# Where a unit's maxima are rounded, and when a weight may be split

## The chip, the cores and the metric

The kernel runs on one core of one Trainium2 chip. The metric is the device time of one execution in microseconds (us). Before the change three runs took 2253.95 us in the median (2253.94 to 2255.15).

The core's engines run side by side, each through its own queue in order. The profile calls them PE (TensorE, matrix products), PEld (its weight loads), DVE (VectorE), ACT (ScalarE), POOL (GpSimd) and SP (SyncE, which issues most transfers here).

## The reference

One input `x` of 2048 tokens by 576 goes through two branches whose results a gate mixes:

```python
g = sigmoid((x * gate_w).sum(-1, keepdims=True))
# branch A: attention with 32 heads of 18
q, k, v = split(x @ wqkv)
p = softmax(q @ k.T * 18 ** -0.5)          # per head, 2048 x 2048
a = concat(p @ v) @ wo
# branch B: a feed-forward block of width 4608
h = gelu(layernorm(x) @ w1 + b1)           # the tanh form of GELU
b = h @ w2 + b2
out = g * a + (1 - g) * b
```

All of it is float32. TensorE multiplies in a shorter float32 form here (`F32R`), so the kernel carries most operands as two parts: `hi`, the value rounded to that form, and `lo`, the remainder `value - hi`. A product is then hi x hi + hi x lo + lo x hi. Making the two parts of a weight is called splitting it.

## The kernel before

After a first stage (projections of q, k, v; layer norm; about the first 250 us) one long loop runs. It weaves attention and feed-forward together on TensorE.

**Attention.** Two heads make a pair, half of the queries of a pair make a unit: 32 units, each of 16 steps `kc` over the keys. Before a unit's scores can go through the exponential, the maximum of each query's scores must be known. So every unit is gone through twice. In *rounds* (`s1_round`, 32 to a unit, lines 204 and 206) TensorE makes scores and VectorE reduces each 128x512 bank to its maxima (tile `m4`). When a unit's last round has been issued, `s1_finish` (lines 209 to 237 with its inner `rows`) reduces the maxima once more to 128x16 negated values `nm` (line 215), makes the rounded part `nmh` (216), copies it beside the remainder into `nm2` (217, 218), and two slots later `rows` transposes `nm2` (222) and stores it in two extra rows of the unit's query tile `qa`. The second pass (`s2`, line 279) multiplies with those rows, so that scores come out with the maximum taken off, and ScalarE puts them through `Exp` (line 281). `s2` works in half-steps: two score matmuls, one for each head, into a pool `ps_s2` of two banks, and two exponentials that empty them. `pv` (line 308) multiplies the probabilities with v. Rounds run ahead of `s2`: a unit's rounds are done some four steps (a step is about 3.7 us) before its own second pass begins.

**Feed-forward.** Tokens are worked in four blocks of 512, and for each block the width in 36 chunks of 128, as 18 pairs, nine groups of two pairs. `h_pair` (matmuls of line 547) makes a pair's hidden values, which then go through GELU in pieces on three engines: ScalarE and VectorE empty the banks (572, 571), ScalarE squares (635), GpSimd multiplies (line 160, a helper through which all GpSimd arithmetic of the loop goes), ScalarE takes the tanh (628), GpSimd multiplies again, rounds (tile `hh`) and makes the remainder (tile `hl`). `open_pairs[0]` is 1 from the end of a pair's matmuls until the last of these instructions has been issued; the last matmul of the next pair isn't issued before (line 559). `out_pair` (matmuls of line 679) multiplies with `w2` and VectorE adds the results up (653). The order of a group is: first pair, the outputs of the group before, second pair, and so on.

**Weights.** In the first token block, w1 and w2 come from memory and are split on the way: ScalarE copies into the rounded part (line 444), GpSimd subtracts (line 160, tile `w`), and both parts are stored to scratch memory for the three later blocks, which only load them. `split` appends a job to the list `bg`. w1 comes as 128x1152 per pair through one raw buffer, w2 as 128x576 per chunk through four. After a split the next raw load is issued three slots later.

**What sets the order.** Nothing reorders the instructions; each engine runs what was issued in the order of the program text. A planner in the text decides that order: `run_due` advances a slot, with an estimated time (`now[0]`), issues what was deferred to this slot (`later`, `timed`), and then looks through `bg`: a job starts when GpSimd's estimated backlog is under its bound (one slot's 950 ns for w1, four for w2) and its `due()` is reached, which among other things is no earlier than 12 slots after a w1 load. `fill` puts feed-forward matmuls between half-steps and then calls `run_due`. A round normally runs inside a half-step of `s2`; `lend_round` runs it inside an output tile instead (within a fill), and the next half-step then has none. `take_round` defers `s1_finish` by one slot.

## Time and profile before

| | before |
|---|---|
| median of three runs | 2253.95 us |
| the profiled execution | 2255.1 us, span 2253.3 us |
| busy: PE, DVE, ACT, POOL | 99%, 74%, 64%, 42% of the span |
| granted clock of TensorE | 0.998 |

The span is the stretch from the first to the last instruction of one profiled execution. A row of a timeline reads: start in us, how long in us, engine, line (L281 is line 281 of the kernel), operation, tiles written and read, shape, how many were merged, and in brackets how long the engine stood still before it and what ended that. A row of grouped instructions has the count behind an x, then busy us, mean ns of one, idle us before them. A busy TensorE is not TensorE at its peak, and idle time of an engine that others don't wait for costs nothing.

### The profile page before, as it was taken

The page shows a single profiled execution, that of the slowest core. Times are in us where ns is not written, and L with a number is a line of the kernel's source. Part 1 is how long each engine was busy: PE and PEld are TensorE (multiplying, and loading weights), DVE is VectorE, ACT ScalarE, POOL GpSimd, SP SyncE. Part 2 cuts the span into 40 slices and gives each one's busy share as a digit, 9 for nine tenths or more (in the row PEclk, how much of TensorE's full clock was granted, in tenths as well). Part 3 has the DMA queues.
Part 4 walks back from the last instruction along what each step waited for, and adds up shares of the span by engine and source line. Part 5 has one row for each costly group of instructions (what it writes and reads, how often), then busy time and mean ns, then how long its engine had stood idle before and what let it go on. Part 6 is the DMA issues. An engine that isn't in the chain of part 4 may idle for free.

```text
span 2253.3 us, 51099 instructions
## 1 busy us (share of the span) xinstructions
PE 2231.5 (99%) x20569; PEld 1649.5 (73%) x20569; DVE 1671.8 (74%) x2953; ACT 1431.6 (64%) x2623; POOL 946.2 (42%) x936
## 2 busy tenths in 40 slices
PE   8999999999999999999999999999999999999999
PEld 7878766777777777777777777777777777777769
DVE  5675877777787787778777877787778777877545
ACT  4223677777776666666666666666666666666661
POOL 4002466666664444443444344434444444444420
PEclk9999999999999999999999999999999999999999
DMA  7755655545473424243264424243465233323355
GB/s 244 261 189 184 193 164 164 173 131 163 133 223 137 149 98 126 98 128 108 89 177 153 120 97 131 90 122 120 122 167 159 98 120 115 106 99 115 109 177 193
DMA packets 163218, 323.61 MB, mean 144 GB/s; under 512 B 59646, under 2 KB 86178, under 8 KB 152146
## 3 DMA queue, kind: packets, MB, share of 16 engines
q1 hardware_dynamic: 158982, 313.57, 44.0%
q10 hardware_dynamic: 4000, 6.78, 0.8%
q8 instruction: 162, 2.65, 0.5%
q14 instruction: 74, 0.61, 0.1%
HBM read 229.07 MB, written 95.16 MB: 144 GB/s over the span
## 4 chain that ended last, share of the span: by engine, by line
PE 92%; POOL 3%; DVE 2%; ACT 2%; DMA 1%; issue 0%; SPq 0%; ACTq 0%; DVEq 0%; POOLq 0%
PE ps L308 20%; PE ps L679 19%; PE ps L547 18%; PE ps L279 14%; PE ps L204 11%; PE ps L955 4%; PE ps L1263 3%; PE ps L973 2%; POOL zz L160 1%; POOL hl L160 1%; POOL w L160 1%; DVE m L206 1%; PE ps L870 0%; DMA p<-in_A_wqkv_dram 0%; ACT p L281 0%
## 5 line engine op out<-in xcount | busy, mean ns | idle before, releaser
L206 DVE TENSOR_REDUCE m<-ps 128x1 f32<-128x512 f32 x2048 | 1301.1, 684 | 299.6 <-PE ps L204 254.4
L281 ACT ACTIVATE p<-ps 128x512 f32<-128x512 f32 x1368 | 743.5, 596 | 377.5 <-PE ps L204 231.3
L279 PE MATMUL ps<-qa,ka 56*128 56x512 f32 x2048 | 715.1, 414 | 4.8 <-ACT p L281 3.8
L204 PE MATMUL ps<-ka,qa 54*128 54x512 f32 x2048 | 647.2, 418 | 3.8 <-DVE m L206 2.6
L679 PE MATMUL ps<-w,hh 64*128 64x288 f32 x4352 | 526.2, 296 | 2.4 <-ACT z L572 1.6
L279 PEld LDWEIGHTS ps<-qa,ka 56*128 56x128 f32 x2048 | 359.8, 185 | 229.6 <-issue 113.5
L547 PE MATMUL ps<-big,w 64*128 64x512 f32 x3888 | 513.9, 390 | 0.2 <-ACT vt L984 0.2
L160 POOL TENSOR_SCALAR zz<-zz 128x512 f32<-128x512 f32 x272 | 168.8, 621 | 776.5 <-ACT zz L635 693.9
L281 ACT ACTIVATE ring<-ps 128x512 f32<-128x512 f32 x680 | 369.6, 596 | 190.4 <-PE ps L204 124.9
L547 PEld LDWEIGHTS ps<-big,w 64*128 64x128 f32 x3888 | 401.6, 185 | 51.9 <-ACT vt L984 0.4
L679 PEld LDWEIGHTS ps<-w,hh 64*128 64x128 f32 x4352 | 421.7, 186 | 15.9 <-ACT z L572 2.1
L160 POOL TENSOR_TENSOR zz<-zz,z 128x512 f32<-128x512 f32 x280 | 361.4, 1291 | 34.5 <-ACT zz L637 10.5
L679 PE MATMUL ps<-w,hl 64*128 64x288 f32 x2176 | 364.8, 292 | 0.0
L204 PEld LDWEIGHTS ps<-ka,qa 54*128 54x128 f32 x2048 | 333.5, 185 | 30.0 <-DVE m L206 10.4
L308 PE MATMUL ps<-p,vt 128*32 128x512 f32 x2736 | 344.5, 598 | 0.0
L679 PEld LDWEIGHTS ps<-w,hl 64*128 64x128 f32 x2176 | 246.4, 185 | 1.4
L160 POOL TENSOR_TENSOR w<-x,w 128x576 fp32r<-128x576 f32 (+1 forms) x34 | 69.0, 2033 | 295.7 <-ACT w L444 276.5
L308 PEld LDWEIGHTS ps<-p,vt 128*32 128x32 f32 x2736 | 71.4, 109 | 153.9 <-issue 147.9
L308 PE MATMUL ps<-ring,vt 128*32 128x512 f32 x1360 | 179.1, 598 | 0.0
L160 POOL TENSOR_TENSOR hl<-zz,hh 128x512 fp32r<-128x512 f32 x134 | 172.5, 1287 | 15.2 <-ACT hh L598 4.3
L653 DVE SCALAR_TENSOR_TENSOR x<-ps,x 128x288 f32<-128x288 f32 x270 | 110.8, 452 | 83.3 <-PE ps L679 80.9
L955 PE MATMUL ps<-big,wqk 128*128 128x512 f32 x504 | 121.5, 396 | 0.4 <-ACT wqk L863 0.4
(118 smaller groups left out, 1382.8 us busy)
## 6 DMA issues: line engine op xcount, KB each, us to landing
w<-w_scr SPq DMA_DIRECT2D x54, 1152.0 KB
w<-w_scr SPq DMA_DIRECT2D x108, 576.0 KB
w_scr<-w SPq DMA_DIRECT2D x18, 1152.0 KB
w_scr<-w SPq DMA_DIRECT2D x36, 576.0 KB
qa<-qk_scr SPq DMA_DIRECT2D x192, 72.0 KB
ka<-qk_scr SPq DMA_DIRECT2D x90, 144.0 KB
x<-in_B_w_dram SPq DMA_DIRECT2D x34, 288.0 KB
qk_scr<-hh SPq DMA_DIRECT2D x36, 256.0 KB
```

Of the source, the lines that this page charges most:

```text
L160: fn(*args, **kw)
L204: nc.tensor.matmul(ps, qa[r0:r0 + 54, t * P:(t + 1) * P], ka[r0:r0 + 54, kb * TB:(kb + 1) * TB], start=True, stop=True)
L206: nc.vector.tensor_reduce(M4[u][:, h, t, kb:kb + 1], ps, axis=AX.X, op=ALU.max)
L279: nc.tensor.matmul(ps, ka[r0:r0 + 56, kc * P:(kc + 1) * P], qa[r0:r0 + 56, qb * TB:(qb + 1) * TB], start=True, stop=True)
L281: nc.scalar.activation(RING[n % 3][:, qb, h], ps, AF.Exp, scale=SCALE)
L308: nc.tensor.matmul(OB[u][r:r + 32, :], v[:, k, 19 * h:19 * h + 32], RING[c % 3][:, qb, h, :], start=(k == 0), stop=(k == NT - 1))
L547: nc.tensor.matmul(ps[h], wt[w_][r, c, :], Y[s_][r, c, :], start=(k == 0), stop=(k == 26))
L653: nc.vector.scalar_tensor_tensor(dst, ps[nn][:, :ND], 0.5, b2b[:, cs[nn]] if base else dst, op0=ALU.mult, op1=ALU.add)
L679: mm = nc.tensor.matmul(ps[nn][:, :ND], h_[r, tok], w_[p_][r, cs[nn]], start=(k == 0 or bare and k == 3 * G), stop=(k == 6 * G - 1 or bare ...
L955: nc.tensor.matmul(ps, w_[:, c, ms], big[:, s_, :], start=(k == 0), stop=(k == len(prods) - 1))
L973: nc.tensor.matmul(ps[:, :ND], big[:, s_, tok], w_[:, c, cs], start=(k == 0), stop=False)
L1263: nc.tensor.matmul(ps[t, n][:, :ND], OT[b][3][:, s_, tok], w_part(w_, c)[:, cs], start=(c == 0 and k == 0), stop=(c == 4 and k == 1))
```

## The change

Two things are edited. In `s1_finish`, the rounding of the maxima and the copy into `nm2` go from VectorE to ScalarE; ScalarE also writes the negated rounded part beside the maxima, and the remainder is made in `rows`, two slots later, by a VectorE reduction that adds these pairs, in place of the subtraction. In `split`, a job's `due()` holds it back in the loop while `open_pairs[0]` is 1, beside the slots in which a GELU activation was issued.

```diff
     def s1_finish(u):
 
         m4 = M4.pop(u)
-        nm = asm.tile([P, 2, 8], F32, name="nm")
+        nm = asm.tile([P, 2, 2, 8], F32, name="nm")
         nm2 = asm.tile([P, 2, 2, 8], F32, name="nm2")
         nmh = asm.tile([P, 2, 8], F32R, name="nmh")
-        nc.vector.tensor_reduce(nm, m4, axis=AX.X, op=ALU.max, negate=True)
-        nc.vector.tensor_copy(nmh, nm)
-        nc.vector.tensor_copy(nm2[:, :, 0, :], nmh.bitcast(F32))
-        nc.vector.tensor_tensor(nm2[:, :, 1, :], nm, nmh.bitcast(F32), op=ALU.subtract)
+        nc.vector.tensor_reduce(nm[:, 0], m4, axis=AX.X, op=ALU.max, negate=True)
+        nc.scalar.activation(nmh, nm[:, 0], AF.Copy)
+        nc.scalar.activation(nm[:, 1], nmh.bitcast(F32), AF.Copy, scale=-1.0)
+        nc.scalar.activation(nm2[:, :, 0, :], nmh.bitcast(F32), AF.Copy)
 
         def rows():
             mr = asm.tile([P, 32], F32, name="mr", bufs=1)
+            nc.vector.tensor_reduce(nm2[:, :, 1, :], nm.rearrange("p k a b -> p a b k"), axis=AX.X, op=ALU.add)
             nc.vector.transpose(mr, nm2.rearrange("p a b c -> p (a b c)"))
...
             def due():
-                if looped[0] and aside[0] == slot[0] or raw == (1, 3) and (0, 2) not in HT:
+                if looped[0] and (aside[0] == slot[0] or open_pairs[0]) or raw == (1, 3) and (0, 2) not in HT:
                     return slot[0] + 1
                 return LOADED.get(raw, slot[0] + 1)
```

## The prediction

> **What bounds the kernel now.** I read the page's engine line first, then the stretches of the loop, then what TensorE waits for, the chain of waits, and last the timelines around the places that the edits touch.

> ```profile
> PE 2231.5 (99%) x20569; PEld 1649.5 (73%) x20569; DVE 1671.8 (74%) x2953; ACT 1431.6 (64%) x2623; POOL 946.2 (42%) x936
> ```

> TensorE works 99% of the span: a microsecond in which it stands still is a microsecond of the result, and work taken off VectorE (74%) is worth nothing by itself. The stretches (us, then busy time of PE, PEld, DVE, ACT, POOL):

> ```profile
> 300.00:600.00 300.00, 296.62 (x2876) 213.38 (x2874) 229.01 (x398) 221.06 (x398) 194.37 (x173) 1.00 0.49 153
> 1300.00:1600.00 300.00, 300.00 (x2966) 218.24 (x2964) 236.32 (x413) 200.42 (x372) 124.54 (x131) 1.00 0.32 105
> ```

> Only the early part, where the first token block's weights are split (70 us more on POOL in 300 us), lets TensorE idle: 3.4 us there, none later, at the same clock. Those are the waits of TensorE (us in total, times, longest), and of ScalarE, for 300 to 700 and 250 to 700 us:

> ```profile
> PE ps L279 <- ACT p L281: 3.0, 5, 0.6
> PE ps L279 <- ACT ring L281: 1.0, 2, 0.6
> ```

> ```profile
> ACT zz L628 <- POOL zz L160: 8.6, 6, 1.5
> ```

> Score matmuls wait for exponentials, and the exponentials stand behind a GELU's tanh (L628) that waits for POOL, six times. The chain shows why POOL is late:

> ```profile
> 395.31 2.08 PE ps L547 x18
> ...
> 410.48 2.70 POOL w L160
> ...
> 422.07 1.29 POOL zz L160
> ...
> 450.03 2.08 PE ps L547 x18
> ...
> 460.18 0.93 PE ps L547 x8
> ```

> ```profile
> 1382.61 2.08 PE ps L547 x18
> ...
> 1436.24 2.08 PE ps L547 x18
> ```

> A w1 split of 2.70 us stands ahead of two GELUs, and from there the chain stays on POOL until the tanh. A group of four chunks takes 54.72 us here (450.03 - 395.31) and 53.63 later (1436.24 - 1382.61), where nothing is split. How the wait reaches TensorE:

> ```profile
> 423.38 0.63 ACT L628 ACTIVATE zz<-zz 128x512 f32<-128x512 f32 x1 [1.45 <-POOL zz L160]
> ...
> 423.92 1.07 ACT L281 ACTIVATE p<-ps 128x512 f32<-128x512 f32 x2
> ...
> 424.55 0.50 PE L279 MATMUL ps<-qa,ka 56*128 56x512 f32 x1 [0.60 <-ACT p L281]
> ```

> The score banks (`ps_s2`) are two: a half-step's two score matmuls need the two exponentials of the half-step before. So whatever ScalarE has to wait for ahead of an exponential can stop TensorE.

> **The change, part by part.** *1. No split while `open_pairs` is set.* Each of six groups loses its POOL delay of 2.70 us; the tanh waited 1.45 at most, so it no longer waits, and the group should run at the later pace: 54.72 - 53.63 = 1.09 us, six times, **-6.5 us**. What is late next is nothing on this path: later groups run the same GELUs with no wait for POOL and TensorE at 300.00 of 300. The bounds: nothing, if the wait only moves, and -8.6 us, the whole of ScalarE's wait.

> The splits have to go somewhere.

> ```profile
> 432.19 1.29 POOL L160 TENSOR_TENSOR hl<-zz,hh 128x512 fp32r<-128x512 f32 x1
> 434.86 2.69 POOL L160 TENSOR_TENSOR w<-x,w 128x1152 fp32r<-128x1152 f32 x1 [1.38 <-PE ps L308]
> 451.55 1.45 POOL L160 TENSOR_TENSOR w<-x,w 128x576 fp32r<-128x576 f32 x1 [14.00 <-ACT w L444]
> ```

> ```profile
> 337.47 1.17 ACT L444 ACTIVATE w<-x 128x1152 fp32r<-128x1152 f32 x1
> ```

> POOL is empty for 14 us between the group's second w1 split and its first w2 split. The split that stood at 410 takes the place at 434; the one from 434 must wait for its raw weight (one buffer, loaded 3 slots after the last split and taken as landed 12 slots later, some 15 slots or 14 us): about 448, just ahead of the four w2 splits, which keep their place in the first feed-forward pair, when no GELU is open. Each split's three loads and its store go with it on SP's queue, past the w2 loads and stores; what else that queue carries (query and key rows, a unit's rows of maxima) is issued four steps or more ahead of its use. The weights split at 410 are first used at 460.18, those split at 434 at the next group's start (450.03 + 54.72), so both stay in time. The copy of 1.17 us on ScalarE at this place cost nothing at 337. Price 0; if a pair found its weight missing, it would pay copy and remainder, 1.17 + 2.70 = 3.9 us, in up to seven groups.

> *2. The maxima.* The rows by line, with shapes (busy, mean ns):

> ```profile
> L217 DVE COPY nm<-nmh 128x16 f32<-128x16 f32 x32 | 12.1, 377 | 1.1
> ...
> L216 DVE CAST nmh<-nm 128x16 fp32r<-128x16 f32 x32 | 9.6, 299 | 1.1
> ...
> L218 DVE TENSOR_TENSOR nm<-nm,nmh 128x16 f32<-128x16 f32 x32 | 8.1, 254 | 0.0
> ...
> L883 ACT ACTIVATE x<-x 128x256 f32<-128x256 f32 x4 | 1.6, 411 | 0.0
> ...
> L1076 ACT ACTIVATE gate<-glog 128x16 f32<-128x16 f32 x1 | 0.2, 215 | 0.0
> ```

> VectorE loses 0.93 us a unit and gets a small reduction in `rows` (I take 0.2); it is not what TensorE waits for in the loop, so this counts 0. ScalarE gets three 128x16 activations, 3 x 0.215 = 0.65 us; 32 units of that are 21 us on an engine with a third of its time free. But they wait for VectorE's reduction L215, and ScalarE runs in order. `s1_finish` is called one slot after the unit's last round. Where that round was lent to an output tile (`lend_round`, inside a fill), the slot ends with the fill, before `s2` issues the next half-step: the three activations stand **ahead of that half-step's exponentials**. Unit 13 shows it:

> ```profile
> 1030.56 3.89 DVE L206 TENSOR_REDUCE m<-ps 128x1 f32<-128x512 f32 x6 [0.77 <-PE ps L204]
> ...
> 1032.62 0.58 PE L204 MATMUL ps<-ka,qa 54*128 54x512 f32 x2
> ...
> 1033.82 1.09 ACT L281 ACTIVATE ring<-ps 128x512 f32<-128x512 f32 x2 [0.81 <-PE ps L279]
> ...
> 1034.48 0.22 DVE L215 TENSOR_REDUCE nm<-m 128x16 f32<-128x64 f32 x1
> ...
> 1034.82 0.40 PE L279 MATMUL ps<-qa,ka 56*128 56x512 f32 x1
> ...
> 1035.12 0.40 PE L279 MATMUL ps<-qa,ka 56*128 56x512 f32 x1
> 1035.26 1.09 ACT L281 ACTIVATE p<-ps 128x512 f32<-128x512 f32 x2 [0.34 <-PE ps L279]
> ```

> VectorE is behind with six reductions, so L215 ends at 1034.70. Handing over takes 0.04 (first exponential of 423.92 over after 0.60, TensorE at 424.55). ScalarE is through with the three at 1035.39 instead of starting exponentials at 1033.82; the first ends at 1035.99, the second at 1036.48. The matmul of 1034.82 starts at 1036.03, 1.21 late, the one of 1035.12 at 1036.52, 1.40 late. Behind them stand the output product and everything else of TensorE's queue. **1.4 us.** Going through the timelines at all 32 of L215's places, I find the last two L204 alone among output-tile matmuls in 15 units (3 to 7, 12 to 14, 16, 22 to 26, 31): 21.0 us. In six units (2, 11, 20, 21, 28, 30) a feed-forward pair ends there and ScalarE has no gap:

> ```profile
> 913.13 0.69 ACT L572 ACTIVATE z<-ps,b1t 128x512 f32<-128x512 f32 x1
> 913.72 1.07 ACT L281 ACTIVATE p<-ps 128x512 f32<-128x512 f32 x2
> 914.67 1.15 ACT L635 ACTIVATE zz<-z 128x512 f32<-128x512 f32 x2
> 915.91 1.09 ACT L281 ACTIVATE p<-ps 128x512 f32<-128x512 f32 x2
> ```

> ```profile
> 913.26 0.22 DVE L215 TENSOR_REDUCE nm<-m 128x16 f32<-128x64 f32 x1
> ```

> ```profile
> 916.89 0.39 PE L279 MATMUL ps<-qa,ka 56*128 56x512 f32 x1
> ```

> L572 starts at 913.48 + 0.04 + 0.65 = 914.17, 1.04 late, the exponentials of 915.91 some 0.9 late; the matmul of 916.89 gets its bank at 917.42, and with its second half 0.8 us are lost: 4.8 us. In the others (the round ran inside `s2`) the activations fall into idle time of ScalarE: 0.3 in all. Together **+26.1 us**.

> Three activations of this shape in a row, each reading what one before wrote, are not in the trace. Bounds: 0.51 us at VectorE's shortest kind (0.17, L218 undisturbed), 1.23 at the 0.411 of L883. That is 1.26 to 1.98 in the 15 units and 0.65 to 1.4 in the six: +23 to +38 us. I take 0.215, the row of the same shape on the same engine.

> [...]

> The sum: 26.1 - 6.5 = **+19.6 us**. The profiled run took 2255.1 us with a span of 2253.3, so it would take 2274.7; the median of the three is 2253.95, and from there I forecast **2274 us**.

> **The rivals.** (a) *Not slower.* The activations run behind the exponentials of their half-step, not ahead: then they start after 1034.91, fill the 0.35 us to the next ones and delay no bank. Part 2 costs about 0 and part 1 decides: 2253.95 - 6.5 = 2247.5. For it speaks ScalarE's idle third; against it the order of the calls, and that ScalarE takes its queue in order (423.38 above). It decides from a loss under 6.5/15 = 0.43 us a lent unit. (b) *Half is given back.* TensorE's later waits shrink after a stop, as other engines catch up; half of part 2 is 13: 2260.5. Against it: later there are no waits to shrink. (c) *Part 1 brings nothing*, because the tanh waits on, or ScalarE's new wait takes its place: 2253.95 + 26.1 = 2280. The rule might then as well not bite at all; for it speaks that the stop at 424.55 stands in a lent unit. (d) *Weights come late*: 7 x 3.9 = 27 us on top, about 2301, if the single raw buffer makes the second split of a group miss its gap.

> **How the numbers follow.** Forecast 70%, (a) 8%, (b) 8%, (c) 10%, (d) 4%. The forecast's own range by the bounds of both parts is 23 - 8.6 = +14 to 38 - 5 = +33, 2268 to 2287; its upper end needs activations as long as L883's sixteenfold size, so I cut it at 2285. Down it reaches to (b), 2258. A measurement of this kernel tells about 0.2%, 4.5 us, from no change: (a) gives faster 6% and same 2%; a part of (b) that goes further gives same 4%; slower 88%.

> **What would show it.** Right: in the first block the wait of L628 for POOL is gone and no w1 remainder stands between two GELU rows; the group there takes about 53.7 us plus ScalarE's new stops; TensorE's wait for L281 grows from 4 us to over 20, in 15 units right behind small activations of lines 216 to 218, each with VectorE's L215 as its releaser. Wrong: the small activations behind the exponentials (a), TensorE waiting for `w` (d), or L628 still waiting (c). A time under 2258 would make part 2's price wrong.

## The result and the profile after

The changed kernel takes 2274.72 us in the median (2273.75 to 2276.16), the kernel before in the same comparison 2255.34: a ratio of 1.0088, 95% interval 1.0075 to 1.0101, 19.4 us slower. The profiled execution has a span of 2273.2 us.

The engine line, and the two stretches shown of before:

```profile
PE 2243.9 (99%) x20569; PEld 1647.7 (72%) x20569; DVE 1654.6 (73%) x2889; ACT 1442.5 (63%) x2719; POOL 946.5 (42%) x936
```

```profile
300.00:600.00 300.00, 297.49 (x2892) 213.37 (x2890) 227.01 (x391) 221.50 (x414) 191.68 (x172) 1.00 0.45 143
...
1300.00:1600.00 300.00, 298.99 (x2916) 215.90 (x2908) 230.58 (x397) 201.95 (x387) 131.18 (x138) 1.00 0.33 106
```

VectorE lost 17 us of work and ScalarE got 11 more; neither number says anything of the result. TensorE, which did not stand still in the later stretch before, now does: 298.99 of 300. What it waits for, and what ScalarE waits for, over the whole run (us, times, longest):

```profile
PE ps L280 <- ACT p L282: 6.8, 9, 0.8
...
PE ps L280 <- ACT ring L282: 5.4, 7, 0.8
...
PE ps L280 <- DMA qa<-mr: 0.7, 1, 0.7
...
PE ps L548 <- POOL w L160: 0.5, 1, 0.5
```

```profile
ACT nmh L216 <- DVE nm L215: 31.7, 31, 1.7
```

The lines after the new reduction are one further down: the score matmuls are L280, the exponentials L282. TensorE's wait for exponentials went from 4.8 to 12.2 us, all in idle time that the profile can see. A busy TensorE includes the modelled ends of matmuls, so a stop is longer than the idle time: in unit 13, below, 0.80 us of idle time stand for 1.3 us that TensorE comes later. ScalarE waits in 31 of 32 units for VectorE's reduction, a microsecond each.

The timeline of the lent unit that the prediction worked out (unit 13):

```profile
1035.52 3.89 DVE L206 TENSOR_REDUCE m<-ps 128x1 f32<-128x512 f32 x6 [0.76 <-PE ps L204]
...
1037.60 0.58 PE L204 MATMUL ps<-ka,qa 54*128 54x512 f32 x2
...
1039.45 0.22 DVE L215 TENSOR_REDUCE nm<-m 128x16 f32<-128x64 f32 x1
...
1039.70 0.22 ACT L216 ACTIVATE nmh<-nm 128x16 fp32r<-128x16 f32 x1 [1.72 <-DVE nm L215]
1039.95 0.22 ACT L217 ACTIVATE nm<-nmh 128x16 f32<-128x16 f32 x1
...
1040.07 0.20 ACT L218 ACTIVATE nm<-nmh 128x16 f32<-128x16 f32 x1
1040.18 1.06 ACT L282 ACTIVATE ring<-ps 128x512 f32<-128x512 f32 x2
...
1040.81 0.49 PE L280 MATMUL ps<-qa,ka 56*128 56x512 f32 x1 [0.80 <-ACT ring L282]
```

The rounding stands first in ScalarE's queue with nothing to do for 1.72 us, while the score banks of the half-step are full; the exponentials follow, and TensorE gets its bank when the first is over.

On GpSimd the splits went where the prediction put them (the raw weight's copy, then `w`, at 434 and 448):

```profile
430.19 1.30 POOL L160 TENSOR_TENSOR hl<-zz,hh 128x512 fp32r<-128x512 f32 x1
434.00 2.66 POOL L160 TENSOR_TENSOR w<-x,w 128x1152 fp32r<-128x1152 f32 x1 [2.51 <-ACT w L445]
448.61 2.67 POOL L160 TENSOR_TENSOR w<-x,w 128x1152 fp32r<-128x1152 f32 x1 [11.94 <-ACT w L445]
```

And at the stop of before at 424.55, ScalarE's two rows now read:

```profile
422.19 0.63 ACT L629 ACTIVATE zz<-zz 128x512 f32<-128x512 f32 x1
424.03 0.22 ACT L216 ACTIVATE nmh<-nm 128x16 fp32r<-128x16 f32 x1 [1.21 <-DVE nm L215]
```

The tanh no longer waits for GpSimd. The wait that takes its place, in the same gap, is part 2's.

### The profile page after: what moved, and what is told of

Same layout as the page of the kernel before. It is cut to its first block, busy times and chain, and to the rows that moved or that the text cites. A ratio compares the mean times of both kernels' runs of the same rounds, so it can differ in the third digit from the quotient of the medians.

```text
span 2273.2 us, 51149 instructions
## 1 busy us (share of the span) xinstructions
PE 2243.9 (99%) x20569; PEld 1647.7 (72%) x20569; DVE 1654.6 (73%) x2889; ACT 1442.5 (63%) x2719; POOL 946.5 (42%) x936
## 4 chain that ended last, share of the span: by engine, by line
PE 91%; DVE 4%; DMA 3%; ACT 2%; issue 0%; SPq 0%; POOL 0%; ACTq 0%; DVEq 0%
PE ps L309 20%; PE ps L548 19%; PE ps L680 18%; PE ps L280 13%; PE ps L204 11%; PE ps L956 5%; DVE m L206 2%; PE ps L974 2%; PE ps L1264 1%; PE ps L871 1%; DMA ka<-ot_scr 0%; ACT p L282 0%; DMA dn_scr<-dn 0%; DMA x<-ot_scr 0%; PE ps L1005 0%
## 5 line engine op out<-in xcount | busy, mean ns | idle before, releaser
L206 DVE TENSOR_REDUCE m<-ps 128x1 f32<-128x512 f32 x2048 | 1302.6, 684 | 324.5 <-PE ps L204 293.2
L282 ACT ACTIVATE p<-ps 128x512 f32<-128x512 f32 x1368 | 743.1, 596 | 370.0 <-PE ps L204 275.3
L280 PE MATMUL ps<-qa,ka 56*128 56x512 f32 x2048 | 712.7, 415 | 13.4 <-ACT p L282 6.8
L204 PE MATMUL ps<-ka,qa 54*128 54x512 f32 x2048 | 650.5, 418 | 3.6 <-DVE m L206 2.4
L280 PEld LDWEIGHTS ps<-qa,ka 56*128 56x128 f32 x2048 | 359.8, 185 | 246.3 <-issue 100.1
L160 POOL TENSOR_SCALAR zz<-zz 128x512 f32<-128x512 f32 x272 | 168.8, 621 | 799.6 <-ACT zz L636 793.9
L282 ACT ACTIVATE ring<-ps 128x512 f32<-128x512 f32 x680 | 369.2, 595 | 187.3 <-PE ps L204 135.8
L548 PEld LDWEIGHTS ps<-big,w 64*128 64x128 f32 x3888 | 395.1, 185 | 60.1 <-POOL w L160 0.9
L160 POOL TENSOR_TENSOR zz<-zz,z 128x512 f32<-128x512 f32 x280 | 361.4, 1291 | 34.9 <-ACT zz L638 10.5
L680 PE MATMUL ps<-w,hl 64*128 64x288 f32 x2176 | 358.4, 292 | 0.0
L204 PEld LDWEIGHTS ps<-ka,qa 54*128 54x128 f32 x2048 | 336.6, 185 | 29.4 <-DVE m L206 9.4
L160 POOL TENSOR_TENSOR w<-x,w 128x576 fp32r<-128x576 f32 (+1 forms) x34 | 68.3, 2011 | 289.0 <-ACT w L445 286.9
L160 POOL TENSOR_TENSOR hl<-zz,hh 128x512 fp32r<-128x512 f32 x134 | 174.0, 1299 | 15.3 <-ACT hh L599 4.5
```

What stands on the lines that cost most here:

```text
L160: fn(*args, **kw)
L204: nc.tensor.matmul(ps, qa[r0:r0 + 54, t * P:(t + 1) * P], ka[r0:r0 + 54, kb * TB:(kb + 1) * TB], start=True, stop=True)
L206: nc.vector.tensor_reduce(M4[u][:, h, t, kb:kb + 1], ps, axis=AX.X, op=ALU.max)
L280: nc.tensor.matmul(ps, ka[r0:r0 + 56, kc * P:(kc + 1) * P], qa[r0:r0 + 56, qb * TB:(qb + 1) * TB], start=True, stop=True)
L282: nc.scalar.activation(RING[n % 3][:, qb, h], ps, AF.Exp, scale=SCALE)
L548: nc.tensor.matmul(ps[h], wt[w_][r, c, :], Y[s_][r, c, :], start=(k == 0), stop=(k == 26))
```

## The experiments

Both kernels issue the score matmuls in the same order, so the start of each one can be compared in two traces. The difference is a staircase: flat where nothing changes, a step where TensorE stopped longer in one of them. Steps below are read that way.

**Part 1 alone.** Against the kernel before, only the line of `due()` is changed:

```diff
-                if looped[0] and aside[0] == slot[0] or raw == (1, 3) and (0, 2) not in HT:
+                if looped[0] and (aside[0] == slot[0] or open_pairs[0]) or raw == (1, 3) and (0, 2) not in HT:
```

> Part 1 alone: no split while open_pairs is set; the maxima stay on VectorE as before. The prediction's part 1: six waits of a tanh for POOL go, 6.5 us in all: 2255.3 - 6.5 = 2249 us, TensorE's wait for L281 in the first block near 0. Rival (c), part 1 brings nothing: 2255.

Measured: 2250.27 us, ratio to before 0.9979 (0.9971 to 0.9988), 4.7 us faster. The staircase goes down at 315, 370, 425, 479, 534 and 589 us, by 1.0 to 1.3 at each, and stands at -6.5 us after the sixth: the size that the prediction had. Then it goes up twice, by 0.78 at 648 and by 1.04 at 672 us. The first is pair 17's start, the last pair of the first block:

```profile
PE ps L279 <- ACT p L281: 2.6, 2, 1.7
...
PE ps L547 <- POOL w L160: 0.5, 1, 0.5
```

Its weight was split so late that TensorE waited for the remainder. At the second place ScalarE's own queue issues the rows of maxima (`store` uses it while the next block's activations are loaded), and the exponentials behind them come 3.74 us after the last. Before the change it was 2.67 us (first row; the other two are of part 1 alone):

```profile
675.71 0.60 ACT L281 ACTIVATE p<-ps 128x512 f32<-128x512 f32 x1 [2.67 <-DVE m L206]
```

```profile
668.99 1.96 ACTq L114 DMA_DIRECT2D qa<-mr  x2
671.00 0.60 ACT L281 ACTIVATE p<-ps 128x512 f32<-128x512 f32 x1 [3.74 <-DMA qa<-mr]
```

SyncE's queue shows what is new there: the store of that late split, among the loads.

```profile
647.93 2.63 SPq L114 DMA_DIRECT2D big<-y_scr  x4
650.66 0.54 SPq L449 DMA_DIRECT2D w_scr<-w  x1
```

**Part 2 alone.** The changed kernel with the old line of `due()`.

> Part 2 alone: ScalarE rounds and copies the maxima, splits as before. With the changed kernel at 2274.7 and part 1 worth 6.5 us: 2281 us. If part 1 brings nothing (c): 2275. If a stop of part 2 and a stop that part 1 removes fall on the same place, something between.

Measured: 2279.1 us, ratio 1.0106 (1.0093 to 1.0120), 24.1 us slower. With part 1's -4.7 that makes 19.4, what the whole change measures: the two parts add up in the sum.

**The activations one slot later.** Both parts, and ScalarE's three instructions deferred:

```diff
-        nc.scalar.activation(nmh, nm[:, 0], AF.Copy)
-        nc.scalar.activation(nm[:, 1], nmh.bitcast(F32), AF.Copy, scale=-1.0)
-        nc.scalar.activation(nm2[:, :, 0, :], nmh.bitcast(F32), AF.Copy)
+        def rounded_parts():
+            nc.scalar.activation(nmh, nm[:, 0], AF.Copy)
+            nc.scalar.activation(nm[:, 1], nmh.bitcast(F32), AF.Copy, scale=-1.0)
+            nc.scalar.activation(nm2[:, :, 0, :], nmh.bitcast(F32), AF.Copy)
+        if looped[0]:
+            defer(1, rounded_parts)
+        else:
+            rounded_parts()
...
-        defer(2 if looped[0] else 8, rows)
+        defer(3 if looped[0] else 8, rows)
```

> Both parts, but ScalarE's three activations are issued one slot later (and the rows of maxima, too), so in a lent unit they stand behind the exponentials of the half-step, not ahead of them. Waiting at the head of ScalarE's queue is the cause (own theory): the stops in the 15 lent units go, 2249 us (2247 to 2254). Rival: the 21 us of added ScalarE work cost time wherever they stand: 2275. Rival: it is the later rows of maxima that TensorE waits for: above 2275.

Measured: 2256.89 us, ratio 1.0012 (1.0003 to 1.0021). The work is the same as in the changed kernel, and 18 of its 24 us over part 1 alone are gone. In unit 13:

```profile
1031.05 1.09 ACT L288 ACTIVATE ring<-ps 128x512 f32<-128x512 f32 x2 [0.81 <-PE ps L286]
1031.70 0.22 DVE L215 TENSOR_REDUCE nm<-m 128x16 f32<-128x64 f32 x1
1032.02 0.22 ACT L218 ACTIVATE nmh<-nm 128x16 fp32r<-128x16 f32 x1
```

The exponentials go ahead, VectorE finishes meanwhile, and ScalarE waits for nothing. In the lent units the staircase has no step over 0.3 us. The expectation of 2249 was still missed, by 8 us. Part 1 alone had missed it by 1.3 already. On top of that the staircase shows 2.5 us in steps of 0.2 to 0.4 where the activations now meet another busy stretch of ScalarE, 1.6 at 1170 us, where TensorE waits 1.3 for rows of maxima, and 1.3 ahead of 290 us, of which more is said below. So the second rival, late rows, is there, in that one place of the loop and with 0.6 us at its start.

**The wait alone.** On top of part 1 alone, with the maxima on VectorE:

```diff
+        seen = asm.tile([P, 2, 8], F32, name="seen")
+        nc.scalar.activation(seen, nm, AF.Copy)
         nc.vector.tensor_copy(nmh, nm)
```

> Part 1, and the maxima on VectorE as before; added is one 128x16 activation on ScalarE that reads L215's result into a tile that nobody uses. It keeps the wait and a third of the work. Own theory: a lent unit loses 1.4 - 2 x 0.215 = 0.97, the six with a pair's end 0.4: 15 x 0.97 + 6 x 0.4 = 17 us over part 1 alone, 2266 us. Rival, the work sets the cost and not the wait: a third of about 25, 2257. Rival, TensorE is held by what is made of the activations' results: 2249.

Measured: 2268.37 us, ratio 1.0060 (1.0047 to 1.0074): 18 us over part 1 alone. One activation of 0.216 us whose result nobody reads costs three quarters of what the three cost by the medians, and two thirds by the staircase from 290 us on (15.4 of 22.6 us). Its row of waits is that of the changed kernel:

```profile
ACT seen L217 <- DVE nm L215: 31.7, 31, 1.7
```

**The work alone.** The same place, three activations, no wait:

```diff
+        seen = asm.tile([P, 2, 8], F32, name="seen")
+        seen2 = asm.tile([P, 2, 8], F32, name="seen2")
+        ready = ident[:, 0:16].rearrange("p (a b) -> p a b", a=2)
+        nc.scalar.activation(seen, ready, AF.Copy)
+        nc.scalar.activation(seen2, seen, AF.Copy, scale=-1.0)
+        nc.scalar.activation(seen2, seen, AF.Copy)
         nc.vector.tensor_copy(nmh, nm)
```

> Part 1, and the maxima on VectorE as before; added are three 128x16 activations in a row on ScalarE at the same place in its queue, which read a constant tile, so they wait for nothing, and whose results nobody uses. Own theory: in a lent unit they end (1033.01 + 0.65 = 1033.66) before the exponentials can start (1033.82): 0; in the six with a pair's end up to 0.5: 2249 to 2252 us. Rival, the added ScalarE work costs time wherever it comes from: about 2272.

Measured: 2251.3 us, ratio 0.9984 (0.9974 to 0.9994), 1 us over part 1 alone. The same work that waits for nothing is nearly free.

**Six activations.** The changed kernel with three more copies of `nmh` into an unused tile.

> The changed kernel with three more 128x16 activations behind its three, which read the rounded maxima into a tile that nobody uses. This doubles the work and leaves the wait. Own theory by 0.215 us each: 0.65 us more in each of 21 units, 13.6 us over the changed kernel, 2288 us. [...] Rival, the wait alone costs: 2275.

Measured: 2300.39 us, ratio 1.0197 (1.0182 to 1.0212): 25.7 us over the changed kernel, about twice the 13.6 that were expected. The steps of the staircase against the changed kernel are about 0.6 in six of the lent units and in the six with a pair's end, as foreseen, 0.4 in five other units, and 2.2 in eight lent units. Stretches around one of these, and its stop:

```profile
1050.00:1051.20 1.20, 1.19 (x8) 0.74 (x12) 0.48 (x1) 1.10 (x3) 0.00 (x0) 1.00 0.00 1
1051.20:1054.60 3.40, 3.40 (x18) 0.78 (x12) 0.81 (x2) 0.43 (x1) 0.00 (x0) 0.50 0.02 3
1054.60:1058.00 3.40, 3.40 (x42) 3.28 (x42) 2.90 (x5) 2.17 (x4) 0.00 (x0) 0.99 0.01 1
```

```profile
1050.01 0.50 PE L284 MATMUL ps<-qa,ka 56*128 56x512 f32 x1 [1.39 <-ACT ring L286]
```

After a stop of 1.39 us TensorE's granted clock was 0.50 for 3.4 us: 18 matmuls in place of 42. That costs 1.7 us beside the stop. Eight times 1.7 is 13.6 us, and the expectation lacked 12.1.

**Five activations.** Two more than the change has, to see whether the clock does this at shorter stops.

> The changed kernel with two more 128x16 activations behind its three, which nobody uses. With six, eight of the stops (1.39 us each) were followed by 3.4 us at a granted clock of 0.50. Two more make a stop 0.42 us longer than the changed kernel's 0.80, that is 1.22: by 0.215 us each 9 us over the changed kernel, 2283 us, if the clock stays; if stops of 1.2 us halve the clock too, up to 14 x 1.7 us more, 2307.

Measured: 2280.67 us, ratio 1.0113 (1.0099 to 1.0126): 6 us over the changed kernel, with a mean granted clock of 0.999. The stop of unit 13 is now

```profile
1041.90 0.49 PE L283 MATMUL ps<-qa,ka 56*128 56x512 f32 x1 [1.15 <-ACT ring L285]
```

and no clock drop follows it or any other stop in a lent unit. ScalarE's rows show why a lent unit loses only 0.25 to 0.4, less than twice 0.216:

```profile
1040.81 0.20 ACT L218 ACTIVATE nm<-nmh 128x16 f32<-128x16 f32 x1
1040.91 0.20 ACT L220 ACTIVATE seen<-nmh 128x16 f32<-128x16 f32 x1
1041.14 0.21 ACT L221 ACTIVATE seen<-nmh 128x16 f32<-128x16 f32 x1
```

The first of the two added ones, which needs nothing of the one before it, starts 0.10 us after it and overlaps it.

**Pair 5 exempt.** Part 1 alone, with one split allowed under an open GELU as before:

```diff
-                if looped[0] and (aside[0] == slot[0] or open_pairs[0]) or raw == (1, 3) and (0, 2) not in HT:
+                if looped[0] and (aside[0] == slot[0] or open_pairs[0] and raw != (1, 5)) or raw == (1, 3) and (0, 2) not in HT:
```

> Part 1 alone, but the w1 split of pair 5 may run while a GELU is open, as before the change. Part 1 alone loses 0.78 us where pair 17 starts (TensorE waits for w) and 1.04 us some 20 us later. Own theory: both come from pair 17's split being half a group late, because the rule pushed every w1 split one place back; with pair 5 exempt each later split moves one place forward, pair 17 is split a group earlier, and both losses go, for one stop of 0.8 to 1.1 us that comes back at pair 5: 0.7 to 1.0 us under part 1 alone, 2249.4. In the trace: no wait of TensorE for w, and the stop at 676 back to the size it has before the change. Rival, the two losses have other causes: they stay, and the time is 1 us above part 1 alone.

Measured: 2249.58 us, ratio 0.9978 (0.9969 to 0.9987). Against part 1 alone the staircase has three steps over 0.25 us: +0.79 at 315 (pair 5's stop is back; 1.1 with the matmuls right behind), -0.77 at 648 and -1.03 at 672. TensorE's wait for `w` is gone from the list. From 290 us to the end the trace gains 0.6 us; the two times alone could not tell that apart.

**Pair 17's store later.** Part 1 alone, with

```diff
-                defer(4 if looped[0] else 20, lambda: nc.sync.dma_start(scr, t.bitcast(F32)))
+                defer((40 if raw == (1, 17) else 4) if looped[0] else 20, lambda: nc.sync.dma_start(scr, t.bitcast(F32)))
```

> Part 1 alone, but pair 17's split weight is stored 36 slots later than otherwise, behind the 24 loads of the next block's activations instead of among them. Own theory: the store among the loads makes the rows of maxima on ScalarE's queue slow there, 1.04 us: the loss at 671 goes, the 0.78 at pair 17's start stays, 1 us under part 1 alone, 2249.2. Rival, the transfers there are slow whatever stands among them: 2250.3, and the loss at 671 as it is.

Measured: 2249.06 us, ratio 0.9974 (0.9964 to 0.9983). One step against part 1 alone: -1.04 at 672; the 0.78 at 648 stays. The loads now run through without the store, and the rows of maxima are issued 1.17 us earlier than the 668.99 shown above:

```profile
647.81 17.38 SPq L114 DMA_DIRECT2D big<-y_scr  x24
```

```profile
667.82 1.95 ACTq L114 DMA_DIRECT2D qa<-mr  x2
```

This and the two kernels with part 1 alone and with pair 5 exempt are faster than both the kernel before and the changed one, and among each other the same within their intervals.

## Why the prediction was right, and where its parts were off

It said 2274 us by a sum of +19.6; measured are 2274.7 and +19.4. That the two are so close is luck: part 2's steps are 3.5 us smaller than predicted, part 1's gain is 1.8 smaller, and 1.5 us from ahead of the loop, most of which are no price of the change, make up the rest.

*What bounds it* held. TensorE's stops in the loop explain 17.9 of the 19.4 us: VectorE's 17 us less bought nothing, and ScalarE's added work without a wait cost about 1 us.

*Part 1, the stops* (-6.5): right in size and places, -6.5 us after the sixth. *Part 1, the moved splits* ("so both stay in time", "Price 0"): this step failed for one pair of 18. The argument used the steady groups only. Each w1 split moved one place back; for pair 17, the next free place without an open GELU is half a group later. It came 0.5 us too late, TensorE lost 0.78 there, and the split's store fell among the next block's loads, which cost 1.04 more. Exempting pair 5 removed both, moving the store removed the second. So part 1 is worth 4.7 us. Rival (d) happened, once instead of seven times.

*Part 2, lent units* (15 x 1.4 = 21.0): mechanism and place right, shown by taking the wait away (the work alone, about 1 us), taking most of the work away (the wait alone, two thirds to three quarters of the cost) and moving the place (one slot later, no stops in lent units). Measured steps are 1.1 to 1.4 in 14 units, 18.5 together. The fifteenth, unit 7, costs nothing in the end. Its stop is there (0.81 us of idle time), and the staircase rises by 1.4 at 674 us; but at 679, where part 1 alone stops for 1.66 us behind the transfers on ScalarE's queue, the changed kernel stops for 0.40, and the staircase falls by 1.4 again. In part 2 alone, without the late store, it rises by 1.4 and falls by 1.2 there. One sign was sized wrongly: TensorE's wait for exponentials was to grow to over 20 us, and the list above shows 12.2, as the idle time is only part of a stop. The three activations take 0.57 us from the first start to the last end, not 0.65: the first two are 0.216 long and 0.25 apart, the third, which doesn't need the second, overlaps it.

```profile
L216 ACT ACTIVATE nmh<-nm x32: 215/216/218, 239.6 to 2137.9; 128x16 fp32r<-128x16 f32 x32
L217 ACT ACTIVATE nm<-nmh x32: 215/216/217, 239.8 to 2138.1; 128x16 f32<-128x16 f32 x32
L218 ACT ACTIVATE nm<-nmh x32: 198/200/202, 239.9 to 2138.3; 128x16 f32<-128x16 f32 x32
```

The row of the same shape was the right price (0.215), and the gap between reader and writer (0.25 less 0.216, 0.03 us) was left out of it.

*Part 2, units where a pair ends* (6 x 0.8 = 4.8): 0.62 to 0.66 each, 3.9. *The others* (0.3): about 0.2.

*Not in the sum*: at 290 us the changed kernel's trace is 1.7 us behind that of the kernel before. Both are single executions, and most of it is not the change's. The first hidden matmul already starts 1.4 us later, 16 us ahead of the first of the three activations (239.6). The row of before, then that of the changed kernel:

```profile
222.46 0.72 PE L547 MATMUL ps<-big,w 64*128 64x512 f32 x4 [0.18 <-ACT vt L984]
```

```profile
223.88 0.96 PE L548 MATMUL ps<-big,w 64*128 64x512 f32 x6
```

Six and five activations, which hold part 2 as well, start this matmul at 223.49 and 222.21, the wait alone, which does not, at 223.61. No run here shows what sets this difference between the traces. The same holds for 0.9 of the 1.3 us of the activations one slot later (223.78, against 222.85 in part 1 alone). The change itself can add the other 0.3: at the loop's start TensorE now waits 0.7 us for unit 0's rows of maxima (the list above), where it waited 0.6 us for an exponential before.

The terms as measured: 18.5 + 3.9 + 0.2 - 4.7 = 17.9 us. The other 1.5 of the measured 19.4 belong to no term of the sum; the traces show them ahead of 290 us.

*The rivals.* (a) fell with the stops themselves; the activations one slot later are what (a) described, and take 2257, not 2247.5, mainly by part 1's smaller gain, the small steps and the late rows told above. (b) is true of unit 7 alone; everywhere else the staircase is flat between the steps to within 0.1 us. (c) fell with part 1 alone.

## What to carry to other kernels

An instruction on an idle engine isn't free when it waits (here one activation of 0.216 us that waited cost 18 us over 32 units, three that waited for nothing about 1): price it by what is queued behind it and by when its input is ready, not by its own length. Before moving a small step to the engine with time to spare, look at what that engine does next and whether someone's bank or buffer hangs on it; issuing the step behind that work took most of the loss away (18 of 24 us). And when a rule delays work in a repeating pattern, check the last turn of the pattern too (0.78 us here), with the transfers that it drags along (1.04). Last, when two traces are compared, see what part of the difference stands ahead of the first instruction that was changed: here it was 1.4 us.
